# Gathering the first two tiles of the last layer one expert earlier, from five experts' rows

## The chip, the cores and the metric

The kernel runs on one core of a Trainium2 chip. The metric is the time of one execution on the device in microseconds (us), the median of several runs, lower is better. TensorE (PE) multiplies matrices, PEld loads its weights, VectorE (DVE) and ScalarE (ACT) do elementwise work, GpSimd (POOL) issues the indirect transfers, and SyncE (SP) issues most other DMAs.

## The reference

Three layers follow each other. A gated linear attention gives 1536 rows of 384 numbers. A mixture of 8 experts sends each row to one expert. A dense layer follows on all rows. Cut to what matters here:

```python
expert_idx = np.argmax(x @ w_gate, axis=1)
# each row takes the next free place of its expert, in the rows' order
h = np.maximum(np.einsum('ecd,edf->ecf', disp, w1), 0.0)      # 8 experts, 384 -> 1024
y = np.einsum('ecf,efd->ecd', h, w2)                          # 1024 -> 384
out[i] = gate_w[i] * y[expert_idx[i], pos[i]]
...
h = x @ w_in                                                  # 384 -> 2048
g = np.maximum(h, 0.0) + alpha * np.minimum(h, 0.0)
return (g @ w_out).astype(np.float32)                         # 2048 -> 384
```

## The kernel before

The attention and the routing come first, in an order that a planner writes out. What the change touches comes after them.

The function `ffn` computes one expert, or one chunk of the last layer. Its input is transposed and split in a high and a low part, `xh` and `xl`, and each product is made of three matmuls (high by high, low by high, high by low). For each of the 8 blocks `ft` of 128 hidden units (16 in the last layer) PE makes `hp` (line 1271), ACT takes the high part `gh` out of it (L1281), DVE the low part `gl` (L1282), and PE adds the block into the outputs `y` (L1254). The second product runs some blocks behind the first, so a `gh` or `gl` has time until PE comes to it. An expert has 256 places, that is two tiles of 128 rows; the last layer takes the rows in three chunks of four tiles, 512 rows each, with `hp` of 512 columns. Its activation uses the buffers with the tag `gn`: two of them, 512 columns wide, idle until the first chunk starts.

An expert's outputs go to a table in the chip's memory, `ys_d`, by two stores of 128 rows (`store`). The last layer's input is gathered from that table. For the first chunk the rows were sorted by expert beforehand (`places_by_expert`), so its first rows come from the first experts. A tile is gathered by four indirect DMAs, each of which fetches a quarter of a row (96 numbers) for 128 places (`gather_blocks`, `indirect`, L1390); POOL issues them one after the other. DVE then transposes a pair of tiles in blocks of 32 (L1217, `turn_blocks`), ACT copies the high part `xh` (L1225), and DVE subtracts for `xl` (L1226). A pair's gathered rows lie either in a buffer of the tag `rows`, of which there are two, or in two `gn` buffers, a tile each. The call `gather_blocks(dst, i)` reads only the rows of the experts below a bound, and waits only for their stores.

`ffn` calls hooks between the blocks. In expert `e` (counted from 0) the hook `ahead` stands at block 1 (`GA`) and fetches the next expert's rows, and in expert 6 also the first chunk's four tiles. In expert 7 the hook `split_first` turns tiles 0 and 1 at block 2 and tiles 2 and 3 at block 4 (`SPLITS`). Between these, DVE prepares the weights of the last layer. Each piece of them lands as 64-bit numbers in one of two buffers `sw`, is made into 32-bit ones by three instructions (L368, L372, L375, in `piece`), and is split by ACT (L378) and DVE (L379, `wl`). The last of the three frees the `sw` buffer, and SP then issues the next load into it. The framework's scheduler sets the order of the instructions on each engine, within the orders that the kernel forces.

Of the kernel before, what the change touches and what calls it, by code (L numbers as in the profile page):

```python
# [27 lines left out]
NE = 8  # L28
CAP = 384
# [46 lines left out]
CHT = 4  # L76
# [154 lines left out]
def tile_kernel(  # L231
# [695 lines left out]
    def after_scatters(ins):  # L927
        for p in scatters:
            tc.add_manual_dep(ins.ins, p.ins.name, SYNC, reason="every scattered row is there")
# [263 lines left out]
    def work(behind, limit):  # L1193
        if todo and todo[0][0] <= limit:
            piece(*todo.pop(0), behind)
        land()

    def pair_tile(name):
        return fp.tile([P, 2, DM], F32, tag="rows", name=name)

    NB = P // BLK
    QD = DM // NB

    def in_blocks(t):
        return t.rearrange("p (a d) -> p a d", d=QD)

    def blocked(rows):
        dst = in_blocks(pair_tile("blocks").rearrange("p j d -> p (j d)"))
        at = rows.rearrange("(a r) (b d) -> b r a d", r=BLK, b=NB)
        return dst, [nc.sync.dma_start(out=dst[n * BLK:(n + 1) * BLK], in_=at[n]) for n in range(NB)]  # L1210
# [122 lines left out]
    def gather_expert(e):  # L1333
        xh = fp.tile([P, KC, SLOTS], F32R, tag="xh", name="xh")
        xl = fp.tile([P, KC, SLOTS], F32R, tag="xl", name="xl")
        at = xs_d[e * CAP:e * CAP + SLOTS, :]
        if e in DEALT:
            rows, loads = blocked(at)
        else:
            rows = pair_tile("rows")  # L1340
            loads = [nc.sync.dma_start(out=rows, in_=at.rearrange("(j p) d -> p j d", p=P))]
        for ins in loads:
            after_scatters(ins)
        if e == 1:
            second_rows.extend(loads)
        return xh, xl, rows

    def split_expert(e, xh, xl, rows, behind):
        if e in DEALT:
            split_blocks([rows], xh, xl, behind)  # L1350
        else:
            for j in range(SLOTS // P):
                split_rows(rows[:, j], xh, xl, j, behind)
        return xh, xl
# [34 lines left out]
    def indirect(out, in_, at, bound):  # L1389
        return G.indirect_dma_start(  # L1390
            out=out, out_offset=None, in_=in_, in_offset=bass.IndirectOffsetOnAxis(ap=at, axis=0), bounds_check=bound,
            oob_is_err=False,
        )
# [85 lines left out]
    quarters = ys_d.rearrange("r (b d) -> (r b) d", b=NB)  # L1479

    def gather_blocks(dst, i):
        rows = ((NE if i >= CHT else NE - 2) * CAP) * NB
        for a in range(dst.shape[1]):
            n = i * NB + a
            first_gathers.append(indirect(dst[:, a], quarters[0:rows], src[:, n:n + 1], rows - 1))

    def gather_pair(i):
        dst = in_blocks(pair_tile("blocks").rearrange("p j d -> p (j d)"))
        gather_blocks(dst, i)
        return [dst]  # L1490

    def gather_halves(i):
        parts = [in_blocks(fp.tile([P, DM], F32, tag="gn", name="blocks")) for _ in range(2)]
        for m, dst in enumerate(parts):
            gather_blocks(dst, i + m)
        return parts

    chunk0 = {}

    def split_first(j, behind):  # L1500
        if j == 0:
            chunk0["x"] = chunk_tiles(CHT)
        split_blocks(chunk0[j], *columns(chunk0["x"], j), behind)

    land()
    for e in range(NE):
        hooks = {ft: [] for ft in range(FT)}
        nxt = {}

        def ahead(behind, e=e):  # L1510
            if e + 1 < NE:
                nxt[0] = gather_expert(e + 1)
            if e == NE - 2:
                chunk0[0], chunk0[2] = gather_pair(0), gather_halves(2)
            land()

        def turned(behind, e=e):
            nxt[0] = split_expert(e + 1, *nxt[0], behind)

        def store(t, o, e=e):  # L1520
            nc.sync.dma_start(out=ys_d[e * CAP + t * P:e * CAP + (t + 1) * P, :], in_=o)

        hooks[GA].append(ahead)
        if e + 1 < NE:
            hooks[GS[e]].append(turned)
        if e == PLACES_AT[0]:
            hooks[PLACES_AT[1]].append(places_by_expert)
        if e == NE - 1:
            for j, at in enumerate(SPLITS):
                hooks[at].append(lambda behind, j=j: split_first(2 * j, behind))  # L1530
        for ft in range(FT) if e < NE - 1 else EARLY_WIDE:
            if e or ft not in NONE_AT:
                hooks[ft].append(lambda behind, e=e, ft=ft: work(behind, 2 * e + 4 + (ft == FT - 1)))
        ffn(*xe, SLOTS, [e], store, hooks)
        xe = nxt.get(0)
# [84 lines left out]
```

## Time and profile before

| what | value |
|---|---|
| median of 3 runs | 507.93 us (505.71 to 510.11) |
| time of the profiled execution | 506.83 us |
| its span on the core | 504.9 us |
| PE busy | 486.3 us (96%) |
| DVE busy | 349.4 us (69%) |
| ACT busy | 302.8 us (60%) |
| POOL busy | 129.4 us (26%) |

The span runs from the first to the last instruction of one execution; about 2 us of its time lie around it. An engine is busy while an instruction of it runs. Of the chain of work that ended last, 72% is PE's. Times in the trace count from the span's start.

### The profile page before, as it was taken

To read this page: it belongs to the slowest core of one execution; us is meant where nothing else is said; L and a number is where in the kernel's file an instruction comes from. 1 tells how busy PE (TensorE), PEld (TensorE's weight loads), DVE (VectorE), ACT (ScalarE), POOL (GpSimd) and SP (SyncE) were. 2 spreads that over 40 slices of the span, in tenths; PEclk is the share of its full clock that TensorE was granted. 3 is DMA by queue.
4 is the path that set the end of the run, shared out by engine and by line. 5 is a ranking of instruction groups with operands and counts; after the bars stand their busy time and mean duration, and the time that the engine had idled before them with its cause. 6 is when DMAs were issued, how large, how long until landed. Compare 5 with 4: busy or idle time off the path is not lost.

```text
span 504.9 us, 8683 instructions
## 1 busy us (share of the span) xinstructions
PE 486.3 (96%) x3281; PEld 444.0 (88%) x3281; DVE 349.4 (69%) x618; ACT 302.8 (60%) x552; POOL 129.4 (26%) x117
## 2 busy tenths in 40 slices
PE   7899999999999999999999789999999999999993
PEld 7778787788899999999999779989898999899993
DVE  5698999898957678798799589987443453423332
ACT  7898999989634656666654245554444443533341
POOL 0243046254431000000018606268732000200000
PEclk9999999999999999999999979999999999999998
DMA  8855789221234988988856546451015000000002
GB/s 262 276 142 164 225 305 330 71 82 60 74 117 153 337 265 277 258 243 270 305 162 203 161 146 217 141 121 21 13 49 171 20 13 1 31 32 0 1 1 69
DMA packets 44769, 73.07 MB, mean 145 GB/s; under 512 B 12992, under 2 KB 35408, under 8 KB 43952
## 3 DMA queue, kind: packets, MB, share of 16 engines
q1 hardware_dynamic: 41376, 65.64, 41.4%
q0 software_dynamic: 3200, 6.71, 4.4%
q8 instruction: 27, 0.44, 0.4%
q14 instruction: 22, 0.18, 0.1%
q10 hardware_dynamic: 144, 0.10, 0.1%
HBM read 57.45 MB, written 14.97 MB: 143 GB/s over the span
## 4 chain that ended last, share of the span: by engine, by line
PE 72%; ACT 8%; issue 5%; DMA 4%; POOL 4%; DVE 3%; SPq 0%; POOLq 0%; DVEq 0%; ACTq 0%
PE y L1254 30%; PE hp L1271 29%; POOL blocks L1390 3%; PE y L706 2%; PE sc L687 2%; ACT L440 2%; PE u L720 2%; DMA st<-in_moe_w 1%; PE pt L579 1%; PE pqT L667 1%; DMA xs_d<-x,sidx 1%; PE pkT L667 1%; PE px L746 1%; PE pl L528 1%; POOL xs_d L893 1%
## 5 line engine op out<-in xcount | busy, mean ns | idle before, releaser
L1271 PE MATMUL hp<-xh,wh 128*128 128x256 f32 (+1 forms) x336 | 110.8, 332 | 0.0
L1271 PE MATMUL hp<-xh,wl 128*128 128x256 f32 (+1 forms) x336 | 110.2, 330 | 0.0
L1254 PE MATMUL y<-wh,gh 128*128 128x384 f32 x320 | 108.0, 338 | 0.0
L1254 PE MATMUL y<-wl,gh 128*128 128x384 f32 x320 | 107.9, 337 | 0.0
L1271 PE MATMUL hp<-xl,wh 128*128 128x256 f32 (+1 forms) x336 | 107.5, 330 | 0.0
L1254 PE MATMUL y<-wh,gl 128*128 128x384 f32 x320 | 89.8, 339 | 4.0 <-DVE gl L1282 4.0
L1390 POOL DMA_INDIRECT blocks<-ys_d,src x32 | 41.5, 1298 | 133.2 <-PE pt L1231 105.7
L1288 DVE SCALAR_TENSOR_TENSOR gn<-gn,nalp,gp 128x512 f32<-128x512 f32 x48 | 35.9, 748 | 56.6 <-ACT gp L1287 56.6
L379 DVE TENSOR_TENSOR wl<-st,wh 128x768 fp32r<-128x768 f32 (+1 forms) x63 | 67.1, 1065 | 10.0 <-ACT wh L378 9.6
L1286 ACT ACTIVATE gn<-hp 128x512 f32<-128x512 f32 x48 | 28.7, 598 | 67.1 <-PE hp L1271 63.5
L1271 PEld LDWEIGHTS hp<-xh,wh 128*128 128x128 f32 x336 | 63.6, 189 | 5.5 <-ACT xh L1225 0.4
L1271 PEld LDWEIGHTS hp<-xh,wl 128*128 128x128 f32 x336 | 63.7, 190 | 4.5
L1271 PEld LDWEIGHTS hp<-xl,wh 128*128 128x128 f32 x336 | 62.9, 189 | 4.8
L378 ACT ACTIVATE wh<-st 128x768 fp32r<-128x768 f32 (+1 forms) x63 | 58.9, 935 | 9.5 <-DVE st L375 6.5
L1254 PEld LDWEIGHTS y<-wl,gh 128*128 128x128 f32 x320 | 60.5, 189 | 1.7
L1254 PEld LDWEIGHTS y<-wh,gh 128*128 128x128 f32 x320 | 60.5, 189 | 1.6
L1254 PEld LDWEIGHTS y<-wh,gl 128*128 128x128 f32 x320 | 57.2, 189 | 5.1 <-DVE gl L1282 4.2
L1290 DVE TENSOR_TENSOR gl<-gn,gh 128x512 fp32r<-128x512 f32 x48 | 33.1, 689 | 26.3 <-ACT gh L1289 26.3
L1281 ACT ACTIVATE gh<-hp 128x256 fp32r<-128x256 f32 x64 | 24.4, 383 | 44.5 <-PE hp L1271 44.4
L474 POOL TENSOR_TENSOR ai<-ai 128x384 f32<-128x384 f32 x36 | 33.7, 935 | 65.8 <-ACT ai L531 63.9
L1289 ACT ACTIVATE gh<-gn 128x512 fp32r<-128x512 f32 x48 | 30.3, 630 | 25.8 <-DVE gn L1288 24.5
L1282 DVE SCALAR_TENSOR_TENSOR gl<-hp,gh 128x256 fp32r<-128x256 f32 x64 | 27.0, 421 | 12.1 <-ACT gh L1281 11.8
(173 smaller groups left out, 783.5 us busy)
## 6 DMA issues: line engine op xcount, KB each, us to landing
st<-in_moe_w SPq DMA_DIRECT2D x24, 512.0 KB, 5.1
st<-in_moe_w SPq DMA_DIRECT2D x12, 768.0 KB, 6.3
sw<-in_moe_w_in SPq DMA_DIRECT2D x6, 1024.0 KB, 5.0
sw<-in_moe_w_out SPq DMA_DIRECT2D x8, 768.0 KB, 4.6
xs_d<-zero SPq DMA_DIRECT2D x4, 1152.0 KB, 7.1
vt<-in_v SPq DMA_DIRECT2D x12, 256.0 KB, 3.5
st<-in_moe_w SPq DMA_DIRECT2D x8, 384.0 KB, 3.3
ys_d<-o SPq DMA_DIRECT2D x16, 192.0 KB, 3.7
```

The lines of the kernel that those rows point to most:

```text
L378: follow(A(out=wh[:, js], in_=st, func=ACTF.Copy), behind, "A")
L379: follow(V.tensor_tensor(out=wl[:, js], in0=st, in1=wh[:, js].bitcast(F32), op=ALU.subtract), behind, "V")
L474: (V if e == "V" else G).tensor_tensor(out=t, in0=t, in1=t, op=ALU.mult)
L1254: ins = T.matmul(out=ys[t], lhsT=a[:, sl], rhs=b[:, f, :], start=(ft == 0 and m == 0), stop=(ft == nf - 1 and m == 2))
L1271: ins = T.matmul(out=hp, lhsT=a[:, c, fs], rhs=b[:, c, :], start=(n == 0), stop=(n == 3 * KC - 1))
L1281: last["A"] = A(out=gh, in_=hp, func=ACTF.Relu)
L1282: last["V"] = V.scalar_tensor_tensor(out=gl, in0=hp, scalar=0.0, in1=gh.bitcast(F32), op0=ALU.max, op1=ALU.subtract)
L1286: A(out=gn, in_=hp, func=ACTF.Relu, scale=-1.0)
L1288: V.scalar_tensor_tensor(out=gn, in0=gn, scalar=nalp[:, ft:ft + 1], in1=gp, op0=ALU.mult, op1=ALU.add)
L1289: last["A"] = A(out=gh, in_=gn, func=ACTF.Copy)
L1290: last["V"] = V.tensor_tensor(out=gl, in0=gn, in1=gh.bitcast(F32), op=ALU.subtract)
L1390: return G.indirect_dma_start(out=out, out_offset=None, in_=in_, in_offset=bass.IndirectOffsetOnAxis(ap=at, axis=0), bounds_check=bound, o ...
```

## The change

Tiles 0 and 1 of the first chunk are gathered in expert 5, which is the sixth, into the two `gn` buffers, from the outputs of experts 0 to 4 alone. Tiles 2 and 3 stay in expert 6, read experts 0 to 5 as before, and take the `rows` buffer that tiles 0 and 1 had.

```diff
     def gather_blocks(dst, i):
-        rows = ((NE if i >= CHT else NE - 2) * CAP) * NB
+        rows = (NE if i >= CHT else NE - 3 + i // 2) * CAP * NB
...
             if e + 1 < NE:
                 nxt[0] = gather_expert(e + 1)
+            if e == NE - 3:
+                chunk0[0] = gather_halves(0)
             if e == NE - 2:
-                chunk0[0], chunk0[2] = gather_pair(0), gather_halves(2)
+                chunk0[2] = gather_pair(2)
             land()
```

On POOL, at the first gathers of the last layer, the names are those of the buffers: before, 3412 is the `rows` buffer of tiles 0 and 1, and 3437 and 3438 are the `gn` buffers of tiles 2 and 3; after, 3204 and 3205 are the `gn` buffers, of tiles 0 and 1, and 3438 is the `rows` buffer, of tiles 2 and 3; 4074 is that of tiles 4 and 5.

```order
-L1390 DMA blocks_3412<-ys_d_82,src_85 128x96 x8
-L1390 DMA blocks_3437<-ys_d_82,src_85 128x96 x4
-L1390 DMA blocks_3438<-ys_d_82,src_85 128x96 x4
+L1390 DMA blocks_3204<-ys_d_82,src_85 128x96 x4
+L1390 DMA blocks_3205<-ys_d_82,src_85 128x96 x4
+L1390 DMA blocks_3438<-ys_d_82,src_85 128x96 x8
 L1390 DMA blocks_4074<-ys_d_82,src_85 128x96 x8
```

Still 16 gathers stand in a row, and in the same order of tiles; the first eight now wait for the stores of expert 4, the other eight for those of expert 5, where all sixteen waited for those of expert 5.

On DVE in expert 7, from the end of the weight piece `st_3577` to the turning of tiles 2 and 3, before:

```order
L375 SCALAR_TENSOR_TENSOR st_3577<-sw_3527,st_3577 128x1024
L1282 SCALAR_TENSOR_TENSOR gl<-hp,gh 128x256
L372 SCALAR_TENSOR_TENSOR st_3627<-sw_3555,st_3627 128x768
L1282 SCALAR_TENSOR_TENSOR gl<-hp,gh 128x256
L1217 STREAM_TRANSPOSE turned<-blocks 128x768
L379 TENSOR_TENSOR wl_3520<-st_3577,wh_3519 128x1024
L375 SCALAR_TENSOR_TENSOR st_3627<-sw_3555,st_3627 128x768
L1282 SCALAR_TENSOR_TENSOR gl<-hp,gh 128x256
L1226 TENSOR_TENSOR xl<-turned,xh 128x3x256
L368 TENSOR_SCALAR st_3663<-sw_3583 128x768
L1282 SCALAR_TENSOR_TENSOR gl<-hp,gh 128x256
L1217 STREAM_TRANSPOSE turned<-blocks 128x384 x2
```

The same stretch of DVE with the change:

```order
L375 SCALAR_TENSOR_TENSOR st_3577<-sw_3527,st_3577 128x1024
L372 SCALAR_TENSOR_TENSOR st_3627<-sw_3555,st_3627 128x768
L1282 SCALAR_TENSOR_TENSOR gl<-hp,gh 128x256
L1217 STREAM_TRANSPOSE turned<-blocks 128x384 x2
L375 SCALAR_TENSOR_TENSOR st_3627<-sw_3555,st_3627 128x768
L379 TENSOR_TENSOR wl_3520<-st_3577,wh_3519 128x1024
L1226 TENSOR_TENSOR xl<-turned,xh 128x3x256
L368 TENSOR_SCALAR st_3663<-sw_3583 128x768
L1282 SCALAR_TENSOR_TENSOR gl<-hp,gh 128x256
L379 TENSOR_TENSOR wl_3626<-st_3627,wh_3625 128x768
L1282 SCALAR_TENSOR_TENSOR gl<-hp,gh 128x256
L1217 STREAM_TRANSPOSE turned<-blocks 128x768
```

The pair that is turned in two instructions is now the first one; the first `gl` behind it stands behind `xl` and L368 instead of ahead of them, and one `wl` more stands ahead of the second turning.

On DVE in expert 6, around the end of the weight pieces `st_3521` and `st_3549`, before:

```order
L375 SCALAR_TENSOR_TENSOR st_3521<-sw_3206,st_3521 128x1024
L1282 SCALAR_TENSOR_TENSOR gl<-hp,gh 128x256
L375 SCALAR_TENSOR_TENSOR st_3549<-sw_3252,st_3549 128x1024
L1282 SCALAR_TENSOR_TENSOR gl<-hp,gh 128x256
L379 TENSOR_TENSOR wl_3520<-st_3521,wh_3519 128x1024
```

The same place with the change (the two `sw` buffers are there called 3232 and 3278):

```order
L372 SCALAR_TENSOR_TENSOR st_3549<-sw_3278,st_3549 128x1024
L1282 SCALAR_TENSOR_TENSOR gl<-hp,gh 128x256
L379 TENSOR_TENSOR wl_3520<-st_3521,wh_3519 128x1024
L1282 SCALAR_TENSOR_TENSOR gl<-hp,gh 128x256
L375 SCALAR_TENSOR_TENSOR st_3549<-sw_3278,st_3549 128x1024
```

The first of the two L375 has moved ahead of this place, and the second, which frees the buffer for the load of `sw_3555`, now stands behind a `wl` and a `gl`.

## Rows read from the trace of the kernel before

**Rows 1.** Page, part 2: granted clock by slices, tenths of full speed.
```profile
PEclk9999999999999999999999979999999999999998
```
**Rows 2.** What PE waited for, 290 us to the end: total, times, longest.
```profile
PE y L1254 <- DVE gl L1282: 4.0, 1, 4.0
```
**Rows 3.** What PE waited for, 17 to 290 us: the longest.
```profile
PE pt L1153 <- DVE ezs L566: 0.5, 1, 0.5
```
**Rows 4.** Stretches: PE, PEld, DVE, ACT, POOL busy (instructions), clock, DMA share, GB/s.
```profile
292.00:294.00 2.00, 2.00 (x7) 2.00 (x8) 2.00 (x4) 0.00 (x0) 0.00 (x0) 0.50 0.00 0
```
**Rows 5.** Timeline of PE around its wait: start, us, instruction, count, [idle before].
```profile
283.38 0.52 PE L1254 MATMUL y<-wh,gl 128*128 128x384 f32 x2
...
287.48 0.28 PE L1271 MATMUL hp<-xl,wh 128*128 128x256 f32 x1
291.75 1.01 PE L1254 MATMUL y<-wh,gl 128*128 128x384 f32 x2 [3.98 <-DVE gl L1282]
```
**Rows 6.** The chain that ended last, 291 to 301 us: start, us, what.
```profile
291.75 2.29 PE y L1254 x6
294.03 3.44 PE hp L1271 x9
297.47 1.06 PE y L1254 x6
298.53 2.08 PE hp L1271 x9
```
**Rows 7.** Timeline of DVE in experts 6 and 7.
```profile
266.63 1.22 DVE L375 SCALAR_TENSOR_TENSOR st<-sw,st 128x1024 uint32<-128x1024 uint32 x1
...
274.37 0.56 DVE L368 TENSOR_SCALAR st<-sw 128x768 uint32<-128x768 uint32 x1 [0.20 <-DMA sw<-in_moe_w_out]
...
277.71 1.23 DVE L1217 STREAM_TRANSPOSE turned<-blocks 128x768 f32<-128x768 f32 x1
...
280.83 0.42 DVE L1282 SCALAR_TENSOR_TENSOR gl<-hp,gh 128x256 fp32r<-128x256 f32 x1
...
282.50 0.41 DVE L1282 SCALAR_TENSOR_TENSOR gl<-hp,gh 128x256 fp32r<-128x256 f32 x1
285.64 0.70 DVE L1217 STREAM_TRANSPOSE turned<-blocks 128x384 f32<-128x384 f32 x1 [2.73 <-issue]
288.96 0.69 DVE L1217 STREAM_TRANSPOSE turned<-blocks 128x384 f32<-128x384 f32 x1 [2.61 <-DMA blocks<-ys_d,src]
```
**Rows 8.** Timeline of POOL: gathers 1, 6, 9 and 16 of the sixteen.
```profile
262.42 1.83 POOL L1390 DMA_INDIRECT blocks<-ys_d,src  x1 [105.72 <-PE pt L1231]
...
270.49 1.99 POOL L1390 DMA_INDIRECT blocks<-ys_d,src  x1 [0.30 <-issue]
...
276.10 1.00 POOL L1390 DMA_INDIRECT blocks<-ys_d,src  x1 [0.30 <-issue]
...
286.36 1.00 POOL L1390 DMA_INDIRECT blocks<-ys_d,src  x1 [0.31 <-issue]
```
**Rows 9.** Timeline of SP's queue: stores of experts 4 and 5, load of `sw_3555`.
```profile
242.07 0.80 SPq L1521 DMA_DIRECT2D ys_d<-o  x2
...
259.00 0.81 SPq L1521 DMA_DIRECT2D ys_d<-o  x2
...
267.88 0.38 SPq L334 DMA_DIRECT2D sw<-in_moe_w_out  x1
```
**Rows 10.** DMA, 262 to 290 us: packets, MB, share; KB, us to landing.
```profile
q0 software_dynamic: 512, 0.79, 11.3%
...
sw<-in_moe_w_out SPq DMA_DIRECT2D x3, 768.0 KB, 5.2
```
**Rows 11.** Timeline of ACT in expert 6's first blocks.
```profile
256.46 0.38 ACT L1281 ACTIVATE gh<-hp 128x256 fp32r<-128x256 f32 x1 [1.20 <-PE hp L1271]
```
**Rows 12.** Timeline of DVE: last `wl` of the second half's first weights.
```profile
324.84 1.21 DVE L379 TENSOR_TENSOR wl<-st,wh 128x1024 fp32r<-128x1024 f32 x1
```
**Rows 13.** Timeline of PE: the matmul that uses that `wl` first.
```profile
328.88 0.39 PE L1271 MATMUL hp<-xh,wl 128*128 128x512 f32 x1
```

## The prediction

> **What bounds the kernel now.** I read the waits of PE first, since PE is busy for 96% of the span. From 17 us to the end they are next to nothing, with one exception: a single wait of 4.0 us on a `gl` of DVE [rows 2], where no other wait between 17 and 290 us is longer than 0.5 [rows 3]. Around it the reader should see three things. PE's last matmul ahead of the wait starts at 287.48, and the next one at 291.75 [rows 5]. DVE is late because of the turning of tiles 2 and 3: it stands still for 2.73 us ahead of the first half and 2.61 ahead of the second, 5.34 in all, and both halves wait for gathered rows [rows 7]. POOL issues the sixteen gathers one by one from 262.42, and the last starts at 286.36, 2.60 ahead of the transpose that uses it [rows 7, 8]. So for this one stretch the end is set by POOL's gathers, through DVE, and elsewhere by PE.
>
> The wait costs more than itself. Behind it the granted clock is 0.50, the 1.2 GHz level [rows 4], and it is the only slice of the page below 9 ahead of the last [rows 1]; what PE did before the fall was to stand still. In the chain, six `y` matmuls then take 2.29 us and nine `hp` 3.44, while the next six and nine take 1.06 and 2.08 [rows 6]. That is 5.73 - 3.14 = 2.6 us lost to the clock. The place costs 4.0 + 2.6 = 6.6 us.
>
> **The gathers.** Before, all sixteen wait for expert 5's stores: these are issued at 259.00, and the first gather starts at 262.42, 3.4 us later [rows 8, 9]. The row names a PE instruction as its releaser, but POOL's buffer was free long before, and I take the stores' landing. Now the first eight need only expert 4's stores, issued at 242.07 [rows 9], and should start at about 245.5. Eight gathers took 276.10 - 262.42 = 13.7 us [rows 8], so they end near 259, and even at the slowest row, 1.99 + 0.30 each, at 263.8. The other eight start as the first one did, at 262.4 (or 263.8), and the last of them starts 13.7 - 1.3 = 12.4 us later, at 275, and is usable 2.6 us after that, at 277.5. DVE wants tiles 0 and 1 at 277.71 and, by the new order, tiles 2 and 3 one `wl` later than the 282.9 at which it was first ready for them (282.50 + 0.41), at about 284 [rows 7]. The first are there with 14 us or more to spare, the second with 6, so the two stalls of DVE, PE's wait and the fall of the clock go: -6.6 us. No instruction is added or dropped; the first pair is now turned in two halves, 0.70 + 0.69 instead of 1.23, which is counted below.
>
> **The queues that they pass.** POOL has nothing else between the routing and these gathers, so nothing is queued behind the earlier wait. SP's order is unchanged. Sixteen gathers took 512 packets and 11.3% of 28 us, 3.2 us of the DMA engines [rows 10], so eight bring 1.6 us of transfers into 245 to 259 us, where weights are being loaded. If a load is late by all of that, ACT's copy of it stands ahead of a `gh`; there ACT still waits 1.20 us for PE [rows 11], and the `gh` has a block or two of time beyond that. I take 0, with 0 to 0.4 as bounds.
>
> **DVE's new order.** This is the term I am least sure of, since without the stall DVE has no slack left in expert 7. In expert 6, the L375 that frees a `sw` buffer stands one `wl` (1.21) and one `gl` (0.42) later than before, when it ran at 266.63 and SP issued the next load at 267.88 [rows 7, 9, 12]. By these durations the load goes out at 269.5, and with 0.8 more for waits on ACT at 270.3. It lands 5.2 us later by the median [rows 10], or 6.5 by what the row at 274.37 had to wait for [rows 7]: between 274.7 and 276.8, against 274.37 now. Behind it stand, in the new order, a `gl`, L375, L372, a `gl` and the turning of tiles 0 and 1, in before's rows 277.71 - 274.37 = 3.3 us [rows 7]. So this turning starts between 277.9 and 280.1.
>
> From there to the first `gl` DVE has the transposes, L375, `wl`, `xl` and L368. In before the same work with one `gl` among it took from 277.71 to 282.50, 4.79 us [rows 7]; less that `gl` and plus 0.16 for the halves, 4.5. So this `gl` ends between 282.8 and 285.0. PE uses it at 283.38: the `gl` of 280.83 is the one that PE takes there, two uses ahead of the one that it waits for at 291.75 [rows 5, 7]. PE then waits between 0 and 1.6 us. I take 0.4, near the lower end, because the median landing is nearer to the rows than the one landing that shared the engines with a larger load. A wait of 0.5 left the clock at 9 in every slice [rows 1, 3], so no fall comes with it. The later `gl`s and the `xl` of tiles 2 and 3 have at least 1 us each by the same count.
>
> **The sum.** -4.0 - 2.6 + 0.4 = -6.2 us: 506.83 - 6.2 = 500.6 for an execution like the profiled one. That one lies 0.2% below the median of 507.93, and the same share of the median is 501.7 us, 1.2% faster. A change of about 1% is what runs of this kernel, 505.71 to 510.11, can tell from none.
>
> **Rivals.** First, the wait moves instead of going. PE stands at the first `gl` of expert 7 for the full 1.6 us, since DVE is then busy without a gap, and the clock falls again for 2.6. For it: the new order puts two instructions ahead of that `gl`, and a load is freed later. Against it: the clock has no second fall in the rows, and 1.6 needs the latest landing. It leaves 6.6 - 1.6 - 2.6 = 2.4 us: 504.4, or 505.5 by the median.
>
> Second, DVE becomes the bound of the first chunk. PE would come 6.6 us earlier, but DVE gains only the 5.34 that it stood still, less what it is late, up to 2.4. The tightest place that I found is the last `wl` of the second half's weights, done at 324.84 + 1.21 = 326.05 and used at 328.88, 2.8 us of slack [rows 12, 13]. At worst 6.6 - (5.34 - 2.4) = 3.7 us of it are asked for, and PE waits 0.9; with a fall of the clock 3.5. The time is 501.5 to 504.1, or 502.6 to 505.2 by the median. Against it: DVE also waits for PE at the start of that chunk, so an earlier PE gives part of this back.
>
> Third, on the other side: gathers that get slower. The eight of tiles 2 and 3 start at 262.4 as now, and must land by the second turning at about 284, so the point at which this decides is (284 - 2.6 - 262.4) / 8 = 2.4 us a gather. Above it DVE stands still again. At 4.0 us, twice the slowest of the sixteen rows, the last is usable at 262.4 + 32 + 2.6 - 1.3 = 295.7; PE went on 291.75 - 288.96 = 2.8 us behind the second half's start [rows 5, 7], so here at 298.5, and PE, free at 287.6, loses 10.9 + 2.6 = 13.5 in place of 6.6: 513.7, or 514.8 by the median. The quickest of the rows takes 1.00 and the slowest of the sixteen 1.99 [rows 8], which speaks against it; for it speaks only that none of them ran beside the work of 245 to 259 us.
>
> The Trainium skill, "SBUF — State Buffer", section "SBUF: two separate sides", states such a mechanism: while DVE runs an instruction in a two-port mode, GpSimd cannot write the descriptors of its DMAs, and the transfer starves. By that rule gathers can stretch wherever DVE copies or converts between SBUF tensors, as L368 does. The trace bears it out only as far as a spread of two to one, and this spread is in the sum already.
>
> Fourth, that the change doesn't do what it says: the second eight wait for their `rows` buffer, and the wait stays whole, at 506.8 (507.9 by the median). Against it: the first gather of before filled the same buffer in the same expert and started at 262.42 [rows 8].
>
> **How the numbers follow.** Forecast 0.62, first rival 0.18, second 0.10, third 0.05, fourth 0.05. The low end is the lowest of the runs shown less the whole 6.6: 499.1. The high end takes in the first two rivals: 505.5. That leaves out the last two and what scatter adds. Faster by over 1%, below 502.85: most of the forecast (0.55 of 0.62), and a little of the first two rivals, 0.60 in all. Slower by over 1%: the third rival and scatter, 0.06. The rest is 0.34.
>
> **What would show it.** POOL's first gather starts near 245.5, its ninth near 262.4. DVE has no wait of over 1 us ahead of either turning. PE's wait of 4.0 on `gl` is gone and no slice of the clock but the last lies below 9. If instead PE waits at a `gl` near 283 us, the first rival is right; if it waits in the first chunk with the clock down, the second; if the gathers take over 2.4 us each, the third. I would be wrong altogether if the clock fell in a new place for a reason that no row of before shows.

## The result and the profile after

The changed kernel takes 500.72 us (500.28 to 501.43, 4 runs) beside 507.55 for the kernel before on the same chip (505.71 to 510.11, 4 runs): a ratio of 0.986, interval 0.982 to 0.991. On a second chip it took 500.34 (500.09 to 501.99, 6 runs) beside 508.36 (502.98 to 509.90, 22 runs), ratio 0.986 again, 0.982 to 0.990. Ratios are those of the means to the kernel before on the same chip, with their 95% interval; one more run of before, 511.46 us, was in a slower state of the chip and is left out. The profiled execution is of 500.46 us, 6.37 less than that of before.

The page of the changed kernel, the line of PE in part 1 and the granted clock in part 2:

```profile
PE 484.1 (97%) x3281; PEld 442.8 (89%) x3281; DVE 348.8 (70%) x618; ACT 303.4 (61%) x552; POOL 133.8 (27%) x117
...
PEclk9899999999999999999999999999999999999997
```

The slice of 7 near 295 us [rows 1] is gone. The 8 at the start lies at 12 to 15 us, far ahead of the change; at expert 4's stores both kernels are level again (242.11 us, and 242.07 in [rows 9]).

What PE waited for, the longest of 17 to 290 us and the longest of 290 us to the end (total, times, longest):

```profile
PE pt L1153 <- DVE ezs L566: 0.5, 1, 0.5
...
PE hp L1271 <- ACT xh L1225: 0.2, 1, 0.2
```

The wait of 4.0 [rows 2] is gone. What is left is 0.2 us at the second chunk's first `hp`, at some 353 us.

The stretch of 292 to 294 us (columns as in [rows 4]), and the timeline of PE at the place of the old wait:

```profile
292.00:294.00 2.00, 2.00 (x11) 1.65 (x10) 2.00 (x3) 1.31 (x2) 0.00 (x0) 1.00 0.81 193
```

```profile
283.31 0.51 PE L1254 MATMUL y<-wh,gl 128*128 128x384 f32 x2
...
287.53 0.51 PE L1254 MATMUL y<-wh,gl 128*128 128x384 f32 x2
...
288.58 0.39 PE L1271 MATMUL hp<-xh,wh 128*128 128x512 f32 x1
...
291.72 0.39 PE L1271 MATMUL hp<-xh,wh 128*128 128x512 f32 x1
```

The two products that waited until 291.75 [rows 5] now start at 287.53, with no idle time ahead of them. They and the 19 matmuls behind them, up to the next block's first `hp` at 291.72, take 4.19 us. Before, the same 21 went from 291.75 to 298.37, 6.62 us, at a clock of 0.50 until about 297 us. The row of before at which that count ends:

```profile
298.37 0.39 PE L1271 MATMUL hp<-xh,wh 128*128 128x512 f32 x1
```

Timeline of POOL: gathers 1, 8, 9 and 16 of the sixteen, and the two slowest of tiles 4 and 5.

```profile
246.63 1.58 POOL L1390 DMA_INDIRECT blocks<-ys_d,src  x1 [89.54 <-DVE gl L1282]
...
256.38 1.08 POOL L1390 DMA_INDIRECT blocks<-ys_d,src  x1 [0.30 <-issue]
262.63 1.31 POOL L1390 DMA_INDIRECT blocks<-ys_d,src  x1 [5.17 <-DVE gl L1282]
...
273.56 1.00 POOL L1390 DMA_INDIRECT blocks<-ys_d,src  x1 [0.30 <-issue]
...
303.39 3.83 POOL L1390 DMA_INDIRECT blocks<-ys_d,src  x1 [0.30 <-issue]
307.53 3.83 POOL L1390 DMA_INDIRECT blocks<-ys_d,src  x1 [0.30 <-issue]
```

The second eight start where the first eight did before, and the last of the sixteen starts 12.8 us earlier than in [rows 8].

Timeline of DVE: L368 that waits for a weight load, the turning of tiles 0 and 1, the first `gl` behind it, and the turning of tiles 2 and 3.

```profile
274.40 0.55 DVE L368 TENSOR_SCALAR st<-sw 128x768 uint32<-128x768 uint32 x1
...
277.53 1.28 DVE L1217 STREAM_TRANSPOSE turned<-blocks 128x384 f32<-128x384 f32 x2
...
282.04 0.41 DVE L1282 SCALAR_TENSOR_TENSOR gl<-hp,gh 128x256 fp32r<-128x256 f32 x1
...
283.57 1.20 DVE L1217 STREAM_TRANSPOSE turned<-blocks 128x768 f32<-128x768 f32 x1
```

Neither turning waits, where 2.73 and 2.61 us stood ahead of the halves [rows 7].

SP's queue, the stores of experts 4 and 5 and the load of the weights that the L368 above reads:

```profile
242.11 0.80 SPq L1523 DMA_DIRECT2D ys_d<-o  x2
...
258.63 0.82 SPq L1523 DMA_DIRECT2D ys_d<-o  x2
...
269.71 0.38 SPq L334 DMA_DIRECT2D sw<-in_moe_w_out  x1
```

That load is issued 1.8 us later than in [rows 9], as the new order of DVE had it, and is there 4.69 us later when DVE comes to it.

### The profile page after: what moved, and what is told of

Read it like the earlier page. It is cut to its first block, busy times and chain, and to the rows that moved or that the text cites. A ratio compares the mean times of both kernels' runs of the same rounds, so it can differ in the third digit from the quotient of the medians.

```text
span 498.7 us, 8686 instructions
## 1 busy us (share of the span) xinstructions
PE 484.1 (97%) x3281; PEld 442.8 (89%) x3281; DVE 348.8 (70%) x618; ACT 303.4 (61%) x552; POOL 133.8 (27%) x117
## 4 chain that ended last, share of the span: by engine, by line
PE 70%; issue 8%; ACT 7%; POOL 6%; DMA 4%; DVE 3%; SPq 0%; POOLq 0%; DVEq 0%; ACTq 0%
PE hp L1271 28%; PE y L1254 28%; POOL blocks L1390 3%; PE y L706 2%; PE sc L687 2%; PE u L720 2%; DMA blocks<-ys_d,src 1%; ACT L440 1%; POOL gs_d L1398 1%; PE pt L579 1%; PE pz L1153 1%; PE pl L528 1%; PE pqT L667 1%; PE pkT L667 1%; PE px L746 1%
## 5 line engine op out<-in xcount | busy, mean ns | idle before, releaser
L1390 POOL DMA_INDIRECT blocks<-ys_d,src x32 | 44.8, 1399 | 127.8 <-DVE gl L1282 94.7
```

The source lines that it names most:

```text
L1390: return G.indirect_dma_start(out=out, out_offset=None, in_=in_, in_offset=bass.IndirectOffsetOnAxis(ap=at, axis=0), bounds_check=bound, o ...
```

## The experiments

My theory after the result: the gathers of all four tiles stood behind expert 5's stores, and taking half of them from behind these stores removes DVE's stall, PE's wait and the clock's fall. Rivals: the exchange of buffers or DVE's new order does it; or only a part is the wait, and the clock would have fallen or not whatever PE did. The kernels are cut to the places that they change, and `...` marks lines left out. The first four runs below (the bound alone, the exchange alone, eight gathers more, 22 idle matmuls) were made on one chip beside 507.48 us for the kernel before (26 runs), the others on the second chip of above.

### The bound alone

```diff
-        rows = ((NE if i >= CHT else NE - 2) * CAP) * NB
+        rows = (NE if i >= CHT else NE - 3 + i // 2) * CAP * NB
```

> One part alone: the kernel before, with the bound of five experts for tiles 0 and 1 only. All sixteen gathers stay in expert 6, in the buffers of before. Theory (POOL's late start costs a wait of 4.0 us and 2.6 us of clock): POOL then waits only for its rows buffer, free when the sixth expert's input is split at 254.7, so the first eight run from about 255 to 267 and the other eight, which still need expert 5's stores of 259, follow to 279; usable by 282, ahead of the turning at about 283. PE's wait and the fall of the clock go: 500.5 to 501.5 us. Rival (the new order on DVE or the exchanged buffers bring the gain): this kernel keeps the old order and buffers, so 507 us. Rival (the gathers need the earlier expert too): DVE stands still for part of the 5.3 us, 503 to 505 us.

Measured: 501.36 us (500.47 to 502.18 in seven runs, 505.97 in the eighth), ratio 0.990, 0.987 to 0.993. POOL's first and last gather, DVE's turning of tiles 2 and 3, and PE's wait:

```profile
255.85 1.57 POOL L1390 DMA_INDIRECT blocks<-ys_d,src  x1 [99.51 <-DMA st<-in_moe_w]
...
280.10 1.73 POOL L1390 DMA_INDIRECT blocks<-ys_d,src  x1 [0.30 <-issue]
```

```profile
283.50 0.70 DVE L1217 STREAM_TRANSPOSE turned<-blocks 128x384 f32<-128x384 f32 x1
285.65 0.70 DVE L1217 STREAM_TRANSPOSE turned<-blocks 128x384 f32<-128x384 f32 x1 [1.45 <-DMA blocks<-ys_d,src]
```

```profile
288.44 0.62 PE L1254 MATMUL y<-wh,gl 128*128 128x384 f32 x2 [0.35 <-DVE gl L1282]
```

With DVE's order and the buffers of before, the sixteen gathers end 5.5 us earlier, DVE still waits 1.45 us for tile 3, PE waits 0.35 for a `gl` at 288.44, and the clock stays at 1.00 from 286 to 302 us. The bound brings most of the gain. The rival that the new order or the buffers bring it falls, and so does the one that the earlier expert is needed as well, which asked for 503 to 505 us.

### The exchange alone

```diff
-                chunk0[0], chunk0[2] = gather_pair(0), gather_halves(2)
+                chunk0[0], chunk0[2] = gather_halves(0), gather_pair(2)
```

> The other part alone: the kernel before with the buffers exchanged (tiles 0 and 1 in the two gn buffers, tiles 2 and 3 in the rows buffer), still gathered in expert 6 from six experts' rows. Theory: all sixteen gathers wait for expert 5's stores as before, the last lands at about 289, and PE waits some 4 us with the clock down behind it: 507 to 508 us. Rival (buffers or DVE's new order bring the gain): 501 to 502 us.

Measured: 507.46 us (505.38 to 511.35), ratio 1.001, 0.998 to 1.003. PE's wait in the timeline, a stretch behind it, and POOL's first gather:

```profile
294.77 1.01 PE L1254 MATMUL y<-wh,gl 128*128 128x384 f32 x2 [5.69 <-DVE gl L1282]
```

```profile
296.00:298.00 2.00, 2.00 (x7) 1.81 (x6) 2.00 (x3) 0.84 (x1) 0.00 (x0) 0.50 0.29 43
```

```profile
263.39 2.97 POOL L1390 DMA_INDIRECT blocks<-ys_d,src  x1 [106.53 <-PE pt L1231]
```

Without the lower bound the exchange does nothing: all sixteen gathers still stand behind expert 5's stores (issued at 259.98, the first gather 3.4 us later, as before), PE waits 5.7 us, and the clock falls to 0.50 from 292 to 298.

### The bound beside the whole change, once more

Both kernels again, on one chip.

> The changed kernel once more, beside the bound alone on one chip: 500.7 (500.0 to 501.5) by every theory.

> The kernel before with only the bound of the gathers of tiles 0 and 1 lowered to five experts' rows, once more. Theory (the bound does all of it, the exchange of buffers and the earlier place of the gathers add under 0.5 us): 500.7 to 501.5, its interval meeting that of the changed kernel. Rival (the exchange brings a part of its own, by the waits of 0.4 and 0.8 us that are left in the seventh expert): 501.5 to 502.0, apart from the changed kernel.

Measured: 500.34 (500.09 to 501.99) for the change and 501.52 (500.88 to 502.02) for the bound alone, ratios 0.986 (0.982 to 0.990) and 0.989 (0.985 to 0.992), six runs each. The bound alone, PE's wait in the timeline and DVE's turning of tile 3:

```profile
288.81 0.62 PE L1254 MATMUL y<-wh,gl 128*128 128x384 f32 x2 [0.76 <-DVE gl L1282]
```

```profile
286.00 0.71 DVE L1217 STREAM_TRANSPOSE turned<-blocks 128x384 f32<-128x384 f32 x1 [1.21 <-DMA blocks<-ys_d,src]
```

The medians lie 1.2 us apart, at the lower edge of the rival's range and the upper of my theory's, and the intervals meet. Five of the six runs of the change lie below the lowest of the bound alone, so what the change has beyond the bound, the earlier place with the other buffers and DVE's order, probably brings a part of its own, about 1 us of the 8. It fits that the gathers end at 281.65 + 1.76 = 283.41 in this execution and leave DVE a wait of 1.21 and PE one of 0.76, where the earlier place leaves none. Which of the three parts it is was not tried; the exchange by itself brought nothing.

### More gathers in the changed kernel

Eight gathers more, the same rows again:

```diff
             if e == NE - 2:
                 chunk0[2] = gather_pair(2)
+                gather_blocks(chunk0[2][0], 2)
```

> One suspected cost doubled: the changed kernel, with the eight gathers of tiles 2 and 3 issued twice into the same buffer (the second set fetches the same rows). At 1.53 to 1.71 us a gather from 262.6 the sixteenth starts at 285.6 to 288.3 and is usable 2.6 us later, so the second turning, wanted at 283.57, starts at 288.2 to 290.9 and PE goes on 2.8 us behind it, at 291.0 to 293.7 where it wanted 287.53. Theory: PE waits 3.5 to 6.2 us and the clock falls for 2.6: 507 to 509.5 us, which gives back all of the gain. Rival (the gathers' end is not what DVE and PE wait for): 500.7 us, no change against the changed kernel.

Measured: 504.20 us (502.24 to 505.97), ratio to before 0.993, 0.991 to 0.995. PE's wait, a stretch behind it, and POOL's ninth and last gather:

```profile
290.73 0.62 PE L1254 MATMUL y<-wh,gl 128*128 128x384 f32 x2 [2.17 <-DVE gl L1282]
```

```profile
292.00:294.00 2.00, 2.00 (x12) 1.74 (x11) 2.00 (x5) 0.00 (x0) 0.00 (x0) 1.00 0.00 0
```

```profile
263.48 0.99 POOL L1390 DMA_INDIRECT blocks<-ys_d,src  x1 [5.65 <-DMA ys_d<-o]
...
286.10 1.00 POOL L1390 DMA_INDIRECT blocks<-ys_d,src  x1 [0.30 <-issue]
```

The last gather starts where that of before did [rows 8], but PE waits 2.17 us instead of 4.0: in this order of DVE the awaited `gl` stands directly behind the turning (at 290.30), where before a half of a turning, a `wl` and L372 came first. The granted clock stays at 1.00 behind it. I had expected a longer wait and a fall, so the time was missed by 3 to 5 us. The profiled execution, 503.12 us, is the second fastest of nine, with a mean clock of 0.997; four of 504.20 to 504.29 have 0.992 or 0.993 and the slowest, 505.97, has 0.988. So the clock may have fallen in some of those, and that a wait of 2.17 us leaves it full here is shown for one execution only.

Two gathers more on top of these:

```diff
                 gather_blocks(chunk0[2][0], 2)
+                gather_blocks(chunk0[2][0][:, 0:2], 2)
```

> The changed kernel with ten gathers more in the seventh expert (the eight of tiles 2 and 3 repeated, then those of the first 256 columns of tile 2's place once more, i.e. two), so the last one ends about 288.7 and the turning of tiles 2 and 3 starts about 291.8. DVE now has it behind three gl instead of one, so what waits on PE is the first chunk's first hp, for xh. Theory (gathers 1.3 us apart are paid one for one once the last is later than about 282): that wait is 4.5 to 5.5 us, 505.2 to 506.2 if the clock stays. A wait of over 4 us drops the clock as it did in the kernel before (4.0) and in the swap alone (5.7) and not as with eight gathers more (2.2): another 2.6 us, 507.8 to 508.8. Rival (the length of the wait doesn't decide on the clock): the clock stays, 505 to 506.

Measured: 506.75 us (502.67 to 509.33), ratio to before 0.997, 0.994 to 1.001. PE's wait, and a stretch behind it:

```profile
294.79 1.01 PE L1254 MATMUL y<-wh,gl 128*128 128x384 f32 x2 [3.90 <-DVE gl L1282]
295.59 0.63 PE L1271 MATMUL hp<-xh,wh 128*128 128x512 f32 x1
```

```profile
294.00:296.00 2.00, 1.22 (x3) 1.07 (x4) 2.00 (x4) 1.49 (x3) 0.00 (x0) 0.57 0.02 4
```

The wait is one for a `gl`, not for `xh` as I wrote, and 3.90 long; the clock falls behind it, so the rival that it would stay falls. The low clock lasts only until 297.7: from 294.79 two `y` and five `hp` take 2.92 us, where the kernel with eight gathers more needed 1.60 for them (290.73 to 291.18 and 291.88 to 293.03), so it costs 1.3 us here. Wait and clock are 1.73 + 1.3 = 3.0 us more than with eight. The two profiled executions differ by 4.81 us: 1.4 of it stand there already at expert 4's stores (243.94 against 242.55), so 0.4 is left open. The medians, of two chips, differ by 2.55. The time lies between the two that I wrote down, since the fall was shorter than the one of before. Two of the ten runs, 502.67 and 503.30 us, lie 3 us below the other eight (506.29 to 509.33); what they did was not traced.

### Work in place of the wait

In the kernel before, to hold the clock. First 22 idle matmuls two blocks ahead of the wait:

```diff
         held = []
+        warm = []
...
             n = 0
+            if units == [NE - 1] and ft == 6:
+                idle = pm.tile([P, KC, P], F32, tag="tr", name="idle").rearrange("p c r -> p (c r)")
+                warm.append(last["hp"])
+                for _ in range(22):
+                    ins = T.matmul(out=idle, lhsT=uh[:, 0, 0:P], rhs=wtiles[2 * units[u] + 1][0][:, 0, :], start=True, stop=True)
+                    in_turn(ins, warm)
+                last["hp"] = ins
             terms = ((uh, xh), (ul, xh), (uh, xl))
```

> The cost of the clock by itself: the kernel before with 22 extra matmuls of 384 columns (0.174 us each, 3.8 us together) between the sixth and the seventh hp block of expert 7, into a PSUM buffer that nothing reads. They add no result. DVE still waits for the gathers until 288.96, so PE arrives at the late gl 3.8 us later and finds it nearly done. Theory (4.0 us of wait and 2.6 us of clock are two terms, and the clock falls because PE stands still): the wait stays as filled time and the clock stays at full, 507.5 - 2.6 = 504.9 us. Rival (the clock falls there for another reason): 507.5 us. Rival (the matmuls add to the path): 511 us.

Measured: 509.68 us (506.12 to 512.58), ratio 1.004, 1.0005 to 1.0085. Its longest wait of PE (lines of code stand 1 to 8 lower in this kernel):

```profile
292.77 0.45 PE L1255 MATMUL y<-wh,gl 128*128 128x384 f32 x1 [2.66 <-DVE gl L1290]
```

The clock stayed at 1.00 behind it, but the time did not fall. The idle work stood ahead of two blocks, so their `hp`, and the `gl` made from them, came later too, and 2.66 us of waiting were left. The trial mixes two things and settles nothing on the time.

Then 15 idle matmuls directly ahead of the products that wait, in one chain with them:

```diff
+            if units == [NE - 1] and ft == nf - 1:
+                t6, g6, l6 = held.pop(0)
+                second(t6, g6, l6, ms=(0, 1))
+                idle = pm.tile([P, KC, P], F32, tag="tr", name="idle").rearrange("p c r -> p (c r)")
+                chain = [last["hp"]]
+                for _ in range(15):
+                    in_turn(T.matmul(out=idle, lhsT=uh[:, 0, 0:P], rhs=wtiles[2 * units[u] + 1][0][:, 0, :], start=True, stop=True), chain)
+                second(t6, g6, l6, chain=chain, ms=(2,))
-            if held and held[0][0] < nf - 1 - hold:
+            elif held and held[0][0] < nf - 1 - hold:
```

(`ms` picks which of the three products `second` makes; lines of code stand 2 to 10 lower.)

> The kernel before with 15 matmuls of 128x384 into an idle PSUM tile, placed between the last product of hp of the eighth expert and the two products of y that wait 4.0 us for gl; their results go nowhere. At 0.175 us each they fill 2.6 us of that wait; gathers, DVE and what is waited for stay as before, so the y products still come at about 291.7. Theory (the fall of the clock behind the wait is a cost of its own, 2.6 us, and comes from TensorE standing still): about 1.4 us of waiting is left, the granted clock stays full behind it, and the time is 507.5 - 2.6 = 504.9 (504.0 to 505.7). Rival (the low clock belongs to that place in the program, or nothing is gained by holding it): the clock falls there all the same, 507.5.

Measured: 507.91 us (506.0 to 510.47), ratio 1.001, 0.998 to 1.004. The profiled execution, 510.30 us, is the second slowest of ten. PE's timeline, a stretch in the second chunk, and on POOL the first gather, the first of eight scatters in the first chunk and the gather behind them:

```profile
285.24 0.62 PE L1256 MATMUL y<-wh,gl 128*128 128x384 f32 x2 [2.01 <-DVE gl L1284]
...
289.57 2.77 PE L1299 MATMUL idle<-wh,wh 128*128 128x384 f32 x15
293.89 0.61 PE L1256 MATMUL y<-wh,gl 128*128 128x384 f32 x2 [1.55 <-DVE gl L1284]
...
298.20 0.39 PE L1273 MATMUL hp<-xh,wh 128*128 128x512 f32 x1
...
361.26 0.50 PE L1273 MATMUL hp<-xh,wh 128*128 128x512 f32 x1 [2.06 <-ACT xh L1225]
...
362.58 0.49 PE L1256 MATMUL y<-wl,gh 128*128 128x384 f32 x1
```

```profile
364.00:366.00 2.00, 2.00 (x8) 1.91 (x7) 0.69 (x1) 0.15 (x1) 1.44 (x2) 0.50 0.03 1
```

```profile
262.13 2.96 POOL L1400 DMA_INDIRECT blocks<-ys_d,src  x1 [105.37 <-PE pt L1231]
...
329.53 3.10 POOL L1408 DMA_INDIRECT gs_d<-sent,sidx  x1 [6.74 <-PE hp L1273]
...
346.67 1.36 POOL L1400 DMA_INDIRECT blocks<-ys_d,src  x1 [0.30 <-DVE gl L1292]
```

At the place the theory holds: with idle work in the wait the clock does not fall, and the same 21 matmuls as above take 298.20 - 293.89 = 4.31 us, not 6.62. So here the low clock came from PE's standing still, and it cost 2.3 us. The time of 504.9 did not come, and the trace of this execution shows two reasons. The first gather took 2.96 us here, and PE waited 2.01 at the `gl` ahead already. And in the second chunk `xh` came late: DVE waited 7.13 us for gathered rows, PE 2.06 for `xh`, and the clock fell 1.3 us after PE had gone on, at 362.58. The rows were late because POOL's eight scatters (indirect writes of the gates to `gs_d`) ahead of these gathers ran long: from 329.53 to 346.67, 17.1 us with 0.3 between two, where in the kernel before they went from 329.79 to 342.99, 13.2 us. Whether every execution of this kernel loses its gain there, the one profile does not tell; the idle work also changed the order of the work behind it, so the time stays open as a measure of the clock.

## Why the prediction was right

**The place that bounds.** Right: the gathers' wait behind expert 5's stores set the end here. The bound alone removes it, the exchange alone does not. I had taken the stores as what releases the first gather against its row, which names PE [rows 8]; with eight gathers more, the row of the ninth, which needs expert 5's stores, names these (`DMA ys_d<-o`, 263.48). That both halves waited for gathered rows was likewise read into a row that names only `issue` for the first [rows 7]. It holds: tile 2's last gather started at 280.01 and landed 5.6 us later, at 285.6, and the half started at 285.64.

```profile
280.01 1.77 POOL L1390 DMA_INDIRECT blocks<-ys_d,src  x1 [0.30 <-issue]
```

The 2.6 us from a gather's start to its use was therefore one row's value and no constant: in the profiles before and after the change, landings came 2.4 to 5.7 us after the start. With 7 us to spare this did not matter in the changed kernel; in the bound alone, where the last gather of 280.10 landed 5.4 us later, it is DVE's wait of 1.45.

**The wait of 4.0 us.** The awaited `y` starts 4.2 us earlier, 287.53 against 291.75 [rows 5].

**The clock, 2.6 us.** The same 21 matmuls take 2.4 us less than before, and 2.3 less in the kernel with idle work ahead of them. The term was taken a little too large, and its reason, that PE stood still, is shown by that kernel's profile.

**DVE's new order, +0.4 us.** It came out at 0 in the profiled execution. The load went out at 269.71 as worked out, but DVE reached the L368 behind it at 274.40 without a wait, so it landed within 4.69 us, less than the median of 5.2. Turning began at 277.53, the first `gl` ended at 282.45, and PE took it at 283.31 with 0.86 us to spare. Both ends that I gave, 282.8 and 285.0, lay too late. In the second profile of the changed kernel the whole execution is later, by 1.1 us at expert 4's stores already: the turning starts at 279.64, the `gl` ends at 284.56, and PE takes it at 285.03 with 0.47 to spare. So the term is 0 in both.

**The queues.** The first gather came at 246.63, not 245.5, the ninth at 262.63 as written. The eight in their new place ended at 256.38 + 1.08 = 257.46, not 259: with their gaps they took 11.1 us instead of the 13.7 that I put down, the seven behind the first 0.99 to 1.08 us each. The eight of tiles 2 and 3 took 1.00 to 1.62 each, so the third rival, which needed 2.4 of them, falls. The price of the transfers is 0 to 0.3, inside its bounds: between 254 and 261 us ACT waits for landing weights 1.02, 0.22 and 0.77 us, where it had waited 0.72 once, but it has that time, and PE has no wait between 230 and 290. In the second profile these waits are 2.49 and 1.13, DVE's work that follows is late, and PE waits 0.31 at a `gl` of expert 6, at 267.70. In the six profiles without the early gathers ACT's waits there add up to 0.7 to 1.1 us.

**The sum.** -4.2 - 2.4 = -6.6 us at 292 us, less the 0.2 of the second chunk's `xh`, is -6.4; the executions differ by 6.37 us, and I had -6.2. Part of that closeness is luck: the errors of the terms, -0.2 (wait), +0.2 (clock), -0.4 (DVE's order) and +0.2 (the second chunk's `xh`), partly cancel.

**The step that was off** is the last, from the profiled execution to the median: 500.6 became 501.7 by the 0.2% between the profiled execution of before and its median, and the kernel took 500.72 and 500.34. For this one change the profiled basis would have been the better one. The runs suggest why. Four runs of before spread over 4.4 us where four of the changed kernel spread over 1.2; on the second chip 22 of before spread over 6.9 and six of the changed kernel over 1.9. In the three profiles of other kernels whose sixteen gathers stand behind expert 5's stores as before, the first gather took 2.97, 2.92 and 2.96 us instead of 1.83 [rows 8], and PE lost 5.7 us to the gathers with the exchange alone, 3.8 + 2.66 = 6.5 (idle work and wait) with the 22 matmuls and 2.0 + 2.8 + 1.55 = 6.3 with the fifteen, instead of 4.0. So part of what varies from run to run seems to sit in the stretch that the change empties. Another part lies ahead of it: expert 4's stores go out between 241.78 and 243.94 us in the ten profiles. In which runs of before the wait was long was not seen, so this cause is argued from a few profiles of edited kernels.

**Rivals.** Neither a wait at the first `gl` nor one in the first chunk came; the second has its trace in the 0.2 us at the second chunk, from POOL, not DVE. The fourth falls with the ninth gather's start.

## What to carry to other kernels

In this kernel a transfer that reads a table waits for every store to the rows that its call names: give it the smallest range of rows that can hold its data, then see whether the order of issue lets the early ones go first. (The range leans on the data: the first five experts must hold the 256 rows of tiles 0 and 1, and no run here has a routing in which they don't.) Price a wait of TensorE with the clock behind it, from a stretch that does the same work at full clock. And where a change removes a wait whose length may vary from run to run, the old spread need not carry over to the work that is left; here it did not.

## What was not expected of the hardware

The clock did not follow the length of the wait alone. Waits of 3.90, 3.98 and 5.69 us were followed by a low clock, and waits of 2.01, 2.17 and 2.66 were not; but behind a wait of 2.06, that of 361 us, the clock fell too. Every profile has one more such place, at its start, where PE waits for DVE's `l` until some 10 us. In five profiles that wait is 1.59 to 2.57 us, and the clock is 1.00 from 11 to 16 us; in the other five it is 2.76 to 3.41, and the clock is 0.50 from 12 to 14. It is not the kernel that decides there: the two profiles of the changed kernel have 2.76 and 1.97. What makes the difference was not tried.

The price differs as well. The low clock cost 2.3 to 2.4 us behind the wait of 3.98, and 1.3 behind that of 3.90. At 12 to 15 us in the changed kernel it cost nothing that lasted: before, where the clock stayed full there, PE waited 1.22 us for ACT next, and at expert 4's stores the two are 0.04 us apart.

One indirect gather of 128 places of 384 bytes took between 0.99 and 4.60 us on POOL (the longest at 307.22 in the kernel with fifteen idle matmuls). The eight that moved ran beside an expert in which DVE made only `gl`, `wl`, `xl` and a turning, and took 0.99 to 1.08, the first 1.58. The two of 3.83 ran beside DVE in the first chunk, which had no gap from 300.40 to 310.49 and ran L368, L372 and L375 there. It isn't the lack of gaps alone: DVE had none from 248.64 to 255.12 either, beside gathers of 0.99 to 1.05. The Trainium skill, "SBUF — State Buffer", section "SBUF: two separate sides", says that GpSimd cannot write the descriptors of its DMAs while DVE runs an instruction in a two-port mode. The trace agrees only in part: the gathers are short where DVE makes no weight pieces, but of the eight at 262 to 274 us, beside such pieces, none took over 1.62, and one L368 lasts 0.68 us, far less than the 2.8 that were lost. Which instructions hold a gather up stays open.
